# Attention and a feed-forward block on one core: three units of the first batch change their key layout, their loads and their order

## The chip, the cores and the metric

The kernel runs on one core of a Trainium2 chip. The metric is the device time of one execution in microseconds (us), lower is better. Beside the times there is a profile of one execution, taken by the hardware profiler. In it PE is TensorE's matmul stream and PEld its weight loads, DVE is VectorE, ACT is ScalarE, POOL is GpSimd and SP is SyncE. L190 is line 190 of the kernel before.

## The reference, cut to what matters

Eight sequences of 448 tokens go through attention with 12 heads of 64, and the result through two matrix products with a leaky ReLU between them. All inputs and the output are float32 (f32); the kernel computes in bfloat16 (bf16).

```python
scores = (q @ k.transpose(0, 1, 3, 2)) / sqrt(64)   # q, k, v: 8 x 12 x 448 x 64
attn   = exp(scores - max); attn = attn / (sum(attn) + 1e-9)
x      = (attn @ v).transpose(0, 2, 1, 3).reshape(3584, 768)
h      = x @ w_in                                   # w_in: 768 x 2048
out    = maximum(0.01 * h, h) @ w_out               # w_out: 2048 x 768
```

## The kernel before, in words

A unit is two heads of one sequence, so there are 48 units, six to a sequence (HP = 6). Units 0 to 5 are the first batch. A unit takes these steps.

- Load: q, k and v come from memory. `load_one` (L170) loads one tensor of one unit in f32 through SyncE's queue; `load_soft` (L153, its transfer on L163) loads one tensor of one or two units through GpSimd's queue and turns it into bf16 on the way. `load_w` (L211, L215) loads a slice of the weights, also through GpSimd's queue. Space for early loads comes from `rooms` (L134): slices of tiles that get their real contents only later (`w_in_mix`, `w_mix`, `o`, `deep_mix`, `c`).
- Cast: `cast` (L183) copies the raw tensor to the layout that the engines want: q and k to `qkb` (L190, for the new key layout L193 to L196), v to `v_old` (L198) or `v_sb` (L201 to L203). GpSimd does most casts. `qkb` has three places (unit number modulo 3).
- Turn: `transposes` (L294, matmuls against an identity on L301) brings q and k of a unit into `qkT`; VectorE copies the result out of PSUM (L305).
- Scores: `scores` (L311) multiplies keys by queries, one chunk of keys at a time; a chunk is one PSUM slot of three.
- Exponential: `expo` (L326, L331, L334, L336) runs on ScalarE, one instruction for a chunk.
- Weighted sum: `pv` (L366), through `pairs` (L355) or `weighted` (L340), multiplies the exponentials by v with a column of ones beside it; VectorE then takes the reciprocal of the sums (L374) and multiplies (L375). `x_transposes` (L379) puts the result into `xT` for the feed-forward part.

There are two key layouts. In the old one a unit's 448 keys are four chunks of 112, each with both heads: four exponentials of 112 partitions by 896 elements, 32 matmuls in the weighted sum. In the new one the first 384 keys are three chunks of 128 with both heads, and the last 64 keys of both heads share one chunk of 128 rows, so that its exponential has 448 elements and not 896; the weighted sum has 28 matmuls. Before the change units from HY = 18 on use the new layout and the first three sequences the old one.

The order of the first batch is written out by hand: `first(u)` (L863) for u from 0 to 5, with `supply(u)` (L851) as the list of casts and loads that GpSimd gets in that unit. Engines take their own instructions in order, so this list is GpSimd's order. After the first batch PE starts on the feed-forward part while later units' attention is placed in between: `part` (L416) and `head` (L783) multiply by `w_in` (L424), `mix_w_in` (L462, L473) makes sums of slices of `w_in` on VectorE, and a planner with a cost model (`place`, L1071) puts scores, turns (units 7 and 8 at first) and weighted sums between the products. The weights `w_in` come in three pieces of column blocks of 128: blocks 0 to 3, 4 to 9 and 10 to 15; below they are called piece one, two and three.

Of the kernel before, what the change touches and what calls it, by code (L numbers as in the profile page):

```python
# [16 lines left out]
def kernel(  # L17
# [9 lines left out]
    nc = tc.nc  # L27
# [100 lines left out]
    w_out_v = moe_w_out.rearrange("(ko ki) n -> ki ko n", ki=P)  # L128

    raw = {}  # L130

# [14 lines left out]
    def room(x, new):  # L146
# [4 lines left out]
        return rooms.pop(0)[:n].bitcast(F32).rearrange("p (h so d) -> p h so d", h=2, so=NSC)  # L151

    def load_soft(u, n, which):  # L153
        b, hp = divmod(u, HP)
        hs = slice(2 * hp, 2 * hp + 2 * n)
        for x in which:
            new = x > 0 and u >= HY
            t = room(x, new).rearrange("p h so d -> p (h so d)").bitcast(BF16)
            t = t.rearrange("p (u h so d) -> p u h so d", u=2, h=2, so=NSC)
            for p, so, keys in ((slice(0, D), NSC, slice(0, NSC * D)), (slice(D, P), KC, slice(NSC * D, S))) if new else (  # L160
                (slice(0, SC), NSC, slice(0, S)),
            ):
                nc.gpsimd.dma_start(  # L163
                    out=t[p, :n, :, :so].rearrange("p u h so d -> p (u h) (so d)"),
                    in_=(q, k, v)[x][b, hs, keys].rearrange("h (p so) d -> p h (so d)", so=so),
                )
            for i in range(n):
                raw.setdefault(u + i, {})[x] = t[:, i]

    def load_one(u, x, queue):  # L170
# [6 lines left out]
        raw.setdefault(u, {})[x] = t  # L177

    def load(u, parts=(0, 1, 2)):
        if u < NU and u % 2 == 0:  # L180
            load_soft(u, 2, parts)

    def cast(u, parts=(0, 1, 2), by=nc.gpsimd.tensor_copy):  # L183
        if u >= NU:
            return
        for x in parts:
            f = raw[u].pop(x)
            t = qkb[u % NB]
            if x < 2 and (x == 0 or u < HY):
                by(t[:SC, x].rearrange("p so h d -> p h so d"), f)  # L190
            elif x == 1:
# [4 lines left out]
                by(t[D:, 1, KC, 1], f[:D, 1, KC])  # L196
            elif u < HY:
                by(v_old[:, u % NV, :, :, :D], f)  # L198
            else:
                t = v_sb[u % NV]  # L200
                by(t[:, :2 * KC, :D].rearrange("p (h so) d -> p h so d", h=2), f[:, :, :KC])  # L201
# [9 lines left out]
    def load_w(n=1):  # L211
        for _ in range(n):
            if w_steps:
                o, i = w_steps.pop(0)
                nc.gpsimd.dma_start(out=o, in_=i)  # L215

    load_one(0, 1, nc.sync)
    load_one(0, 0, nc.sync)
# [47 lines left out]

    cast(0, (1,), both)
    cast(0, (0,), both)


# [23 lines left out]
    def transposes(u, bank=None):  # L294
        n = SC if u < HY else P
        t, flat = qkb[u % NB], qkT[u % NQ].rearrange("p i c s -> p (i c s)")[:, :2 * NSC * n]
# [14 lines left out]
    def scores(u, c):  # L311
        ps = next_slot()
        t = qkT[u % NQ]
        sc_t[u, c] = ps
        if u < HY:
            t = t.rearrange("p i c s -> p (i c s)")
# [9 lines left out]
    def expo(u, c):  # L326
        e, ps = e_sb[u % NE], sc_t.pop((u, c))
        n = SC if u < HY else P
        if c < KC:
            e = e[:n, :EM].rearrange("p (j c s) -> p j c s", j=2, c=KC)  # L330
            nc.scalar.activation(e[:, :, c, :], ps[:n, :, :S], AX.Exp, scale=scale)  # L331
        elif u < HY:
            e = e_old[u % NE][:n, :2 * S].rearrange("p (j s) -> p j s", j=2)
# [32 lines left out]
    def pv(u, j, bank=None):  # L366

        bank = next_bank() if bank is None else bank
        ps = bank[:, :NSC * (D + 1)].rearrange("p (q d) -> p q d", q=NSC)
        pairs(u, j, ps)  # L370
        if j == 0:
            x_t[u] = x_pool.tile([SC, NSC, 2, D], BF16, name="x")
        rec = r_pool.tile([SC, NSC, 1], F32, name="rec")
        nc.vector.reciprocal(rec, ps[:SC, :, D:])  # L374
        nc.vector.tensor_mul(  # L375
            x_t[u][:, :, j, :], ps[:SC, :, :D], rec.to_broadcast([SC, NSC, D])
        )

# [472 lines left out]
    def supply(u):  # L851

        for what, n, *parts in {0: [('load', 6, (0, 1)), ('qk', 3), ('v', 1), ('v', 2), ('load', 6, (2,))], 1: [('qk', 4), ('v', 3), ('load', 8, (0, 1))], 2: [('qk', 5), ('v', 4), ('w', 1)], 3: [('qk', 6), ('v', 5), ('w', 1)], 4: [('qk', 7), ('v', 6), ('load', 10, (0, 1)), ('load', 8, (2,))], 5: [('qk', 8), ('v', 7), ('load', 10, (2,)), ('load', 12)]}[u]:
            if what == "qk":
                cast(n, (0, 1))
            elif what == "v":
                cast(n, (2,))
# [5 lines left out]
    def first(u):  # L863
# [33 lines left out]


    transposes(0)
    cast(1, (0, 1), fast)  # L900
    for u in range(HP):
        first(u)
# [343 lines left out]
```

## Time and profile before

| what | value |
|---|---|
| median of 3 runs | 378.51 us (377.97, 378.51, 380.34) |
| the profiled execution, its time | 378.34 us |
| its span, first to last instruction | 376.6 us |
| TensorE clock granted | 0.999 |
| PE, ACT, DVE, POOL busy over the span | 98%, 69%, 68%, 51% |
| read from memory, written | 45.61 MB, 11.01 MB |

A busy share is an average over stages. The first 25 us (the first batch) and the time after it have different limits, so the stages are read apart. The profile says for each instruction what ended the idle time before it, with the sign "<-"; a second column of microseconds is the duration, and durations of pipelined instructions overlap, so that the distance from start to start is what a queue of them costs. A transfer issued by an engine shows there only as the time to issue it.

### The profile page before, as it was taken

How to read it: one execution, taken by the hardware profiler on the slowest of the kernel's cores; microseconds unless marked ns; L12 is line 12 of the kernel's file. 1: busy time of each engine (PE TensorE's matmuls, PEld its weight loads, DVE VectorE, ACT ScalarE, POOL GpSimd, SP SyncE). 2: the span in 40 equal slices, each digit the busy share in tenths (PEclk: the TensorE clock that was granted, in tenths of full speed). 3: DMA queues.
4: the chain of work that ended last, by engine and by line, in shares of the span. 5: the costliest groups of instructions: out<-in, count | busy, mean ns of one | idle time of the engine just before them, and what ended most of it. 6: DMA issues, size and time to landing. Idle time of an engine off the chain costs nothing.

```text
span 376.6 us, 10120 instructions
## 1 busy us (share of the span) xinstructions
PE 369.7 (98%) x4008; PEld 265.7 (71%) x4008; DVE 256.9 (68%) x558; ACT 259.6 (69%) x399; POOL 191.8 (51%) x376
## 2 busy tenths in 40 slices
PE   7999999999999999999999999999999999999996
PEld 3664658756698556996569966599665995679765
DVE  4765858778666867766676665775847775685763
ACT  5997885866768776758766587666787668636721
POOL 7985871986268989624588235792347020000000
PEclk9999999999999999999999999999999999999999
DMA  9999999999499885973869648798455740321123
GB/s 155 200 203 207 191 204 201 156 159 164 93 178 143 114 163 87 197 158 60 157 121 148 144 64 86 170 147 167 61 66 98 143 110 0 79 58 45 42 65 105
DMA packets 99600, 48.08 MB, mean 128 GB/s; under 512 B 64608, under 2 KB 96352, under 8 KB 99552
## 3 DMA queue, kind: packets, MB, share of 16 engines
q0 software_dynamic: 39600, 22.47, 44.6%
q1 hardware_dynamic: 59504, 24.50, 32.6%
q8 instruction: 31, 0.51, 0.6%
q10 hardware_dynamic: 448, 0.47, 0.4%
q14 instruction: 17, 0.14, 0.1%
HBM read 45.61 MB, written 11.01 MB: 150 GB/s over the span
## 4 chain that ended last, share of the span: by engine, by line
PE 94%; DMA 2%; DVE 1%; issue 1%; POOL 1%; ACT 1%; POOLq 0%; ACTq 0%; DVEq 0%
PE g L682 30%; PE g L548 14%; PE sc L548 14%; PE sc L322 7%; PE sc L350 6%; PE g L424 4%; PE sc L319 4%; PE sc L645 4%; PE sc L362 3%; PE g L817 2%; PE sc L343 2%; DMA w_in_mix<-in_v_dram 2%; PE g L362 1%; PE g L301 1%; PE sc L424 1%
## 5 line engine op out<-in xcount | busy, mean ns | idle before, releaser
L331 ACT ACTIVATE e<-sc 128x896 bf16<-128x896 f32 (+1 forms) x144 | 123.6, 923 | 30.7 <-PE sc L322 20.8
L682 PE MATMUL g<-w_out_sb,h 128*128 128x384 bf16 (+1 forms) x440 | 84.1, 325 | 0.0
L682 PEld LDWEIGHTS <-h 128*128 128x128 bf16 x592 | 54.4, 98 | 41.4 <-issue 11.2
L537 ACT ACTIVATE h<-c 128x512 bf16<-128x512 f32 (+1 forms) x72 | 43.1, 610 | 30.2 <-DVE c L563 12.4
L548 PEld LDWEIGHTS <-w_in_sb 128*128 128x128 bf16 x576 | 54.6, 98 | 5.7
L190 POOL COPY qkb<-fq 112x512 bf16<-112x512 bf16 x34 | 23.9, 703 | 41.6 <-DMA qkT<-qkb 32.5
L548 PEld LDWEIGHTS <-w_in_mix 128*128 128x128 bf16 x432 | 40.5, 98 | 3.7
L201 POOL COPY v<-fv 128x384 bf16<-128x384 bf16 x30 | 18.5, 617 | 43.1 <-PE sc L350 40.7
L687 DVE COPY o<-g 128x384 f32<-128x384 f32 x47 | 26.0, 553 | 13.7 <-PE g L682 13.5
L350 PE MATMUL sc<-v,e 128*128 128x65 bf16 x720 | 33.3, 193 | 0.0
L322 PE MATMUL sc<-qkT 64*128 64x448 bf16 (+1 forms) x210 | 32.8, 352 | 0.0
L350 PEld LDWEIGHTS <-e 128*128 128x128 bf16 x720 | 31.1, 98 | 1.3
L974 DVE RECIPROCAL rec<-sc 112x8 f32<-112x8 f32 x42 | 8.7, 207 | 33.6 <-PE sc L350 19.1
L975 DVE TENSOR_TENSOR x<-sc,rec 112x512 bf16<-112x512 f32 x42 | 29.0, 691 | 1.6 <-DVE rec L974 0.2
L548 PE MATMUL g<-xT,w_in_sb 128*128 128x256 bf16 (+1 forms) x216 | 28.5, 268 | 0.0
L548 PE MATMUL sc<-xT,w_in_sb 128*128 128x256 bf16 (+1 forms) x216 | 28.5, 268 | 0.0
L693 DVE TENSOR_TENSOR o<-o,g 128x384 f32<-128x384 f32 x39 | 21.4, 549 | 9.1 <-PE g L682 4.4
L343 PE MATMUL sc<-v,e 128*128 128x130 bf16 x120 | 26.5, 221 | 0.0
L649 DVE TENSOR_TENSOR o<-o,sc 128x192 f32<-128x192 f32 x39 | 13.7, 351 | 17.9 <-PE sc L645 17.9
L682 PE MATMUL g<-w_mix,h 128*128 128x384 bf16 x128 | 24.6, 326 | 0.2 <-DVE o L687 0.2
L163 POOL DMA_DIRECT2D fv<-in_v_dram x32 | 20.1, 641 | 7.7 <-DMA fq<-in_q_dram 3.1
L682 PE MATMUL g<-w_mix,hmix 128*128 128x384 bf16 x112 | 21.7, 326 | 0.0
(149 smaller groups left out, 744.1 us busy)
## 6 DMA issues: line engine op xcount, KB each, us to landing
fq<-in_q_dram POOLq DMA_DIRECT2D x17, 224.0 KB, 5.7
w_out_sb<-in_moe_w_out_dram POOLq DMA_DIRECT2D x4, 768.0 KB, 13.2
out_dram<-o SPq DMA_DIRECT2D x7, 336.0 KB, 3.4
w_in_sb<-in_moe_w_in_dram POOLq DMA_DIRECT2D x2, 1152.0 KB, 12.7
out_dram<-o SPq DMA_DIRECT2D x7, 288.0 KB, 3.4
fk<-in_k_dram POOLq DMA_DIRECT2D x15, 128.0 KB, 5.9
fv<-in_v_dram POOLq DMA_DIRECT2D x15, 128.0 KB, 4.8
out_dram<-o SPq DMA_DIRECT2D x7, 240.0 KB, 3.1
```

Source lines behind the costliest of these rows:

```text
L163: nc.gpsimd.dma_start(out=t[p, :n, :, :so].rearrange("p u h so d -> p (u h) (so d)"), in_=(q, k, v)[x][b, hs, keys].rearrange("h (p so) d ...
L190: by(t[:SC, x].rearrange("p so h d -> p h so d"), f)
L322: nc.tensor.matmul(ps[:, j, :S].rearrange("p (so s) -> p so s", so=NSC), t[p, 1, c], t[p, 0, :, :SC], start=True, stop=True,)
L331: nc.scalar.activation(e[:, :, c, :], ps[:n, :, :S], AX.Exp, scale=scale)
L343: nc.tensor.matmul(ps, e[:, EM + qc * SC:EM + qc * SC + P], vt[:, 2 * KC:].rearrange("p j d -> p (j d)"), start=True, stop=False, skip_gro ...
L350: nc.tensor.matmul(ps[:, j * (D + 1):(j + 1) * (D + 1)], e[:, at:at + P], vt[:, j * KC + c], start=False, stop=(c == KC - 1), skip_group_c ...
L537: nc.scalar.activation(hs[:, m:m + 2, cols], x.rearrange("p (m t) -> p m t", m=2), AX.Prelu, alpha=0.01)
L548: nc.tensor.matmul(ps[:, j * nh:(j + 1) * nh], w[:, kk, ts(j, P)], x[:, kk], start=(first and j == 0 and kk == 0), stop=(kk == KH - 1), sk ...
L682: nc.tensor.matmul(ps[:, cols], x[:, m], w[:, m], start=(first and m == 0), stop=(m == MH - 1), skip_group_check=True,)
L687: by(o[:, at], ps[:, :NW])
L693: nc.vector.tensor_add(o[:, at], o[:, at], ps[:, :NW])
L975: nc.vector.tensor_mul(x, ps[:, :, :, :D], rec.to_broadcast([SC, 2, 2 * NP, D]))
```

## The change: what it does

Units 3, 4 and 5 move to the new key layout (`old(u)` takes the place of `u < HY` in cast, turn, scores, exponential and weighted sum). Their k and v (k of units 3, 4, 5 and v of units 3, 4, 5) are no longer loaded by GpSimd in bf16; SyncE loads them in f32, in two transfers each, into six fixed places, three of which have first to be emptied of q and k of unit 0 and k of unit 1. GpSimd's opening loads shrink from nine tensors and piece one of `w_in` to six tensors; piece one has five column blocks and not four, and is issued in `supply(0)` behind the cast of unit 3's q and two loads. Units 1 to 5 turn the next unit's q and k ahead of the third and fourth scores and of the first weighted sum.

```diff
+    FIRST = 3
+    def old(u):
+        return u < FIRST or HP <= u < HY
...
+    split = ((slice(0, D), NSC, slice(0, NSC * D)), (slice(D, P), KC, slice(NSC * D, S)))
...
+    def load_into(u, x, t):
+        b, hp = divmod(u, HP)
+        for p, so, keys in split:
+            nc.sync.dma_start(
+                out=t[p, :, :so].rearrange("p h so d -> p h (so d)"),
+                in_=(q, k, v)[x][b, 2 * hp:2 * hp + 2, keys].rearrange("h (p so) d -> p h (so d)", so=so),
+            )
+        raw.setdefault(u, {})[x] = t
...
-    for lo, hi in ((0, 4), (4, 10), (10, MD)):
+    for lo, hi in ((0, 5), (5, 10), (10, MD)):
...
+    homes = [x.bitcast(F32).rearrange("p (h so d) -> p h so d", h=2, so=NSC) for x in rooms[:3] + rooms[9:12]]
+    del rooms[9:12]
     load_one(0, 1, nc.sync)
     load_one(0, 0, nc.sync)
     load_one(1, 1, nc.sync)
...
     load_soft(1, 1, (0,))
-    load_soft(2, 2, (0, 1))
+    load_soft(2, 2, (0,))
+    load_soft(2, 1, (1,))
     load_soft(0, 1, (2,))
     load_soft(1, 2, (2,))
-    load_soft(4, 2, (0, 1))
-    load_soft(3, 2, (2,))
-    load_soft(5, 1, (2,))
-    load_w(1)
+    load_soft(4, 2, (0,))
...
     cast(0, (1,), both)
     cast(0, (0,), both)
+    for u, x, y in ((3, 1, 0), (4, 1, 1), (5, 1, 3), (3, 2, 4), (4, 2, 5)):
+        load_into(u, x, homes[y])
...
-        pairs(u, j, ps)
...
+        if old(u):
+            pairs(u, j, ps)
+            x = x_t[u][:, :, j, :]
+        else:
+            n = 2 * (D + 1)
+            for y in range(NP):
+                weighted(u, j * NP + y, bank[:, y * n:(y + 1) * n])
+            x = x_t[u][:, j * NP:(j + 1) * NP].rearrange("p q j d -> p (q j) d")
...
-        ... {0: [('load', 6, (0, 1)), ('qk', 3), ('v', 1), ('v', 2), ('load', 6, (2,))],
-             1: [('qk', 4), ('v', 3), ('load', 8, (0, 1))], 2: [('qk', 5), ('v', 4), ('w', 1)],
-             3: [('qk', 6), ('v', 5), ('w', 1)], ...
+        ... {0: [('q', 3), ('load', 6, (0, 1)), ('w', 1), ('k', 3), ('v', 1), ('v', 2)],
+             1: [('qk', 4), ('load', 6, (2,)), ('v', 3)],
+             2: [('qk', 5), ('load', 8, (0, 1)), ('qk', 6), ('v', 4), ('w', 1)],
+             3: [('v', 5), ('w', 1)], ...
...
         if u >= 2:
             x_transposes(u - 2, next_bank())
-        if u == 1:
+        if u >= 1:
             transposes(u + 1)
-        if u >= 1:
-            pv(u - 1, 0)
         if u > 1:
             scores(u, 2)
             scores(u, 3)
-        if u != 1:
+        if u >= 1:
+            pv(u - 1, 0)
+        if u < 1:
             transposes(u + 1)
...
     transposes(0)
     cast(1, (0, 1), fast)
+    load_into(5, 2, homes[2])
     for u in range(HP):
         first(u)
```

More of the change, by code (lines that the diff above doesn't have):

```diff
@@ L157, in load_soft @@
             new = x > 0 and u >= HY
-            t = room(x, new).rearrange("p h so d -> p (h so d)").bitcast(BF16)
+            t = room(x, new)
+            t = t.rearrange("p h so d -> p (h so d)").bitcast(BF16)
             t = t.rearrange("p (u h so d) -> p u h so d", u=2, h=2, so=NSC)
-            for p, so, keys in ((slice(0, D), NSC, slice(0, NSC * D)), (slice(D, P), KC, slice(NSC * D, S))) if new else (
-                (slice(0, SC), NSC, slice(0, S)),
-            ):
+            for p, so, keys in split if new else ((slice(0, SC), NSC, slice(0, S)),):
                 nc.gpsimd.dma_start(
@@ L188, in cast @@
             t = qkb[u % NB]
-            if x < 2 and (x == 0 or u < HY):
+            if x < 2 and (x == 0 or old(u)):
                 by(t[:SC, x].rearrange("p so h d -> p h so d"), f)
@@ L314, in scores @@
         sc_t[u, c] = ps
-        if u < HY:
+        if old(u):
             t = t.rearrange("p i c s -> p (i c s)")
@@ L327, in expo @@
         e, ps = e_sb[u % NE], sc_t.pop((u, c))
-        n = SC if u < HY else P
+        n = SC if old(u) else P
         if c < KC:
```

15 lines of the change are left out of this document (8 added, 7 removed).

## The prediction

> **What bounds the kernel now.** I read the busy shares first, then busy time by stretches of 5 us, then the timelines of ACT, POOL and DVE over the first 40 us, the groups by form for prices, and last the DMA queues in short windows.
>
> ```profile
> PE 369.7 (98%) x4008; PEld 265.7 (71%) x4008; DVE 256.9 (68%) x558; ACT 259.6 (69%) x399; POOL 191.8 (51%) x376
> DMA  9999999999499885973869648798455740321123
> 10.00:15.00 5.00, 4.61 (x81) 3.07 (x79) 3.49 (x10) 5.00 (x8) 4.81 (x8) 1.00 1.42 197
> 15.00:20.00 5.00, 4.59 (x86) 3.11 (x84) 3.27 (x9) 5.00 (x7) 5.00 (x9) 1.00 1.32 203
> 20.00:25.00 5.00, 4.79 (x96) 3.49 (x93) 3.39 (x10) 5.00 (x7) 3.54 (x7) 1.00 1.40 200
> 25.00:30.00 5.00, 5.00 (x72) 3.01 (x70) 2.79 (x9) 3.77 (x5) 5.00 (x9) 1.00 1.16 211
> ```
>
> The first line is the whole span, the second the DMA engines in 40 slices of 9.4 us, the rest are stretches (busy us of PE, PEld, DVE, ACT, POOL; clock; DMA share; GB/s). ACT is busy 5.00 of 5 us from 10 to 25 us; after that PE is, and stays so to the end. POOL is full from 15 to 20 us, and the DMA engines never rest in the first 100 us. So the first batch ends when ACT has done its exponentials, and all time after it is PE's, unless something is late.
>
> ```profile
> 9.93 2.55 ACT L331 ACTIVATE e<-sc 112x896 bf16<-112x896 f32 x3
> ...
> 25.20 1.01 ACT L334 ACTIVATE c<-sc 112x896 bf16<-112x896 f32 x1
> 26.38 1.72 ACT L331 ACTIVATE e<-sc 112x896 bf16<-112x896 f32 x2 [0.16 <-PE sc L319]
> L331 ACT ACTIVATE e<-sc 128x896 bf16<-128x896 f32 x90 | 76.1, 918 | 20.8 <-PE sc L322 20.8
> L336 ACT ACTIVATE e<-sc 128x448 bf16<-128x448 f32 x30 | 16.5, 552 | 1.6
> ```
>
> ACT's timeline and two groups. From 9.93 to 25.20 us are 19 exponentials, 0.804 us from start to start, without a gap over 0.13. A chunk of 896 elements is 918 ns, one of 448 is 552.
>
> ```profile
> 9.06 0.85 POOL L215 DMA_DIRECT2D w_in_sb<-in_moe_w_in_dram  x1 [0.41 <-DMA w_in_mix<-in_q_dram]
> 11.59 1.17 POOL L190 COPY qkb<-w_in_mix 112x512 bf16<-112x512 bf16 x2
> 27.83 1.17 POOL L190 COPY qkb<-w_mix 112x512 bf16<-112x512 bf16 x2
> 38.04 0.96 POOL L190 COPY qkb<-w_mix 112x512 bf16<-112x512 bf16 x1 [4.23 <-DMA w_mix<-in_q_dram]
> L194 POOL COPY qkb<-fk 128x384 bf16<-128x384 bf16 x30 | 16.9, 565 | 1.5 <-DMA fk<-in_k_dram 1.5
> L195 POOL COPY qkb<-fk 64x64 bf16<-64x64 bf16 x30 | 8.9, 296 | 0.0
> L201 POOL COPY v<-fv 128x384 bf16<-128x384 bf16 x30 | 18.5, 617 | 43.1 <-PE sc L350 40.7 <-DMA fv<-in_v_dram 1.2
> ```
>
> POOL's timeline: the issue of piece one at 9.06, the first casts, the casts of unit 8's q and k (27.83 to 28.94), and the first long wait, 4.23 us for a load, at 38. Two casts in 1.11 us (11.59 to 12.70) are 0.555 us each. The groups are the new layout's copies.
>
> ```profile
> 36.78 0.56 DVE L473 TENSOR_TENSOR w_in_mix<-w_in_sb 128x768 bf16<-128x768 bf16 x1 [2.56 <-DMA w_in_sb<-in_moe_w_in_dram]
> 38.92 0.21 DVE L974 RECIPROCAL rec<-sc 112x8 f32<-112x8 f32 x1 [0.39 <-ACT e L331]
> ```
>
> ```profile
> 30.52 0.40 PE g L301 x8
> ```
>
> DVE's timeline: it waits 2.56 us for piece three of `w_in` and soon after takes a weighted sum out of PSUM. The last line, from the chain of waits, is PE's turn of unit 8.
>
> **Part by part.** *ACT.* Three exponentials of 896 become 448: 3 x (918 - 552) = 1.10 us off the stage that ACT bounds. This is the gain.
>
> *PE.* A chunk with 64 keys of both heads is one matmul and not two, a weighted sum 28 and not 32, turns are 128 wide and not 112. PE has 0.2 to 0.4 us to spare in each 5 us of the batch (rows above); behind it only unit 5's weighted sum is shorter, by at most 4 of 32 matmuls that take 1.03 us together, 0.13. Nothing taken. The turn moved forward (0.51 to 0.57 us for 8 matmuls) holds back scores 3 and 4: in unit 2 they would start at 14.3 and not 14.19, while ACT needs them at 14.70. Cost 0; if ACT's lead were gone, up to 0.5 a unit. It removes three waits of PE for DVE's copy (0.8 us together), of which ACT saw one gap of 0.13. DVE's copy grows from 0.62 to 0.62 x 1024 / 896 = 0.71, hidden in DVE's 1.5 idle us of 5.
>
> *SP.* Twelve more issues of about 0.45 us (rows of SP's three loads) from 4.1 us on. The transposes behind them start only at 39.88, so the queue costs nothing; what they do to the DMA engines is next.
>
> *DMA.* The same bytes are read. Six tensors of 0.229 MB are now written in f32, in 1536 packets for 1344. GpSimd's queue alone moves 1578 packets in 4 us (10 to 14 us), 394 a us, so 3.4 us of engine time goes. SyncE's queue alone moved 174 in the half us from 3.0, 348 a us, and 250 a us over 2 to 4: 4.4 to 6.1 us come. Were reads the limit (394 packets of 1 KB a us for GpSimd), it would be 3.4 again. So 0 to 2.7 us more work for the DMA engines; I take 1.0, by SyncE's own best row.
>
> ```profile
> q0 software_dynamic: 681, 0.34, 88.6%
> q1 hardware_dynamic: 178, 0.17, 23.5%
> q0 software_dynamic: 1578, 0.78, 144.8%
> ```
>
> The first two lines are 4 to 7 us, where both queues had work, the third 10 to 14 us. The new loads start at about 5 us, beside q and k of unit 2 and v of unit 0, which lands at 10.54 and is on the early chain. Ahead of it lie 1120 packets of GpSimd's queue for 1344 (k of unit 3 has left), of which 235 were moved by 5.5 us. If the queues take equal turns for the other 885, as many new packets come between: 2005 for 1344, 661 / 394 = 1.7 us later. At the 4 to 1 of those rows it is 1341, no delay. PE has about 0.25 us of lead there (scores at 12.57 to 12.85, exponential at 13.11), so ACT loses 0 to 1.45 us. I take 0.4, nearer the row.
>
> *POOL.* Each of units 3, 4, 5 needs a memset (198 ns) and three copies for k, 198 + 501 + 230 + 232 = 1.16 us for 0.555, and three for v, 506 + 230 + 234 = 0.97 for 0.555: 3.07 us more by the medians, 4.63 by the means, which hold the time lost beside DVE. The f32 source has no POOL row; the nearest are DVE's casts (420 ns for f32, 290 for bf16 at 512 elements) and POOL's own equal rate an element; I take equal. The three issues saved (0.7 each) lie ahead of 8.7 us. What counts is the queue from piece one to unit 8's cast: 28.94 - 9.06 = 19.88 us, 1.74 of it idle, so 18.14 of work, which becomes 21.2 to 22.8. It now starts with the cast of unit 3's q, as its load lands: 9.0 us if the new loads cost it nothing (the issue at 9.06 waited for it), 437 / 394 = 1.1 later with equal turns. So unit 8's cast ends between 30.2 and 32.9; I take 9.5 + 21.8 = 31.3, nearer the medians. PE turns unit 8 at 30.52 now, and with ACT's 1.10 less 0.4 would come at 29.8. PE waits there: **0.8 us later than before**, between 0.3 earlier and 2.4 later. This holds no wait of POOL's own for a load or for PE.
>
> *Piece three.* POOL issues piece two behind the same longer queue, at about 23 to 26 us and not 19.23. It lands at 31.0 now; less 1.5 us from last byte to landing (v of unit 0 shows that) and 1.18 MB at 205 GB/s, 5.75 us, its bytes start at 23.8. With a longer piece one ahead (0.197 MB, 1.0 us) they could start at 24.8, and with 1.4 us from issue to first bytes they are there at 24.4 to 27.4. So piece three lands 0 to 2.7 us after its 36.75, by the DMA work or by the late issue, whichever is longer; I take 1.0. DVE's sum waits for it; the take-out of PSUM has 0.39 us to spare (38.53 to 38.92) and PE's next scores another 0.3. So PE is 0.7 early to 2.0 late there, with 1.0 it is 0.3 late. It comes after the turn of unit 8 and is less, so it adds nothing.
>
> Sum: ACT's chain reaches the end of the batch 0.7 us early, POOL's queue gives it back and 0.8 more: 378.34 + 0.8 = 379.1 us for the profiled execution, which is 0.17 under the median of the three runs, and I leave the forecast at **379.1**.
>
> The three issues that POOL is spared stand at nothing in this sum, because POOL's timeline shows it idle just there, 0.78 us before 7.98 and 0.41 before 9.06. The Trainium skill (DMA: Bandwidth & Descriptors, Rules for kernel authors) says that spreading transfers over the issuing engines does not help bandwidth, as all use the same 16 engines, and saves issue time alone. By that rule POOL would gain 3 x 0.70 = 2.1 us, unit 8's cast would end at 29.2 and the sum would be the first rival's 377.7. The trace speaks against it here: the time saved falls into a wait.
>
> **The rivals.** *Faster.* POOL keeps up: q of unit 3 lands by 9, the copies run at their medians or faster, and unit 8's cast ends before PE comes. For it: 21.2 us of work from 9.0 is 30.2. Then ACT's 1.10 stands until piece three, whose 0.69 us of slack caps it: 378.34 - 0.69 = 377.7. It decides at 30.5 us, the end of unit 8's cast; against it is POOL's 5.00 of 5 already.
>
> *The new loads are late.* At the slowest shares (178 packets in 3 us, or 281 in the 3 us from 41, beside GpSimd's queue), k of 3, 4, 5 and v of 3 are 1024 packets and need 11 to 17 us from 5.2 on, with 1.5 to land up to 24. POOL comes to v of unit 3 at 16.5 to 18 and stands there, with k of unit 5 behind it; PE then turns unit 5 some 3 us late and ACT starves. Price 2.5 to 5 us: about 382. Against it: the 178 may be a queue that drained, as k of unit 1 had no more; with equal turns v of unit 3 is there by 14. The Trainium skill (same page, Queues, rings and completion order) says that an engine goes round its queues packet by packet and that a packet holds several descriptors. By that rule GpSimd's joined rows get the larger share and the time would be this rival's 382; the 4 to 1 row bears it out only if that queue had not drained.
>
> *The change does not do what it says.* V of unit 0 lands 1.35 us late, ACT's 1.10 is gone at once, and POOL is just in time for PE at its old place: 378.3.
>
> **How the numbers follow.** POOL's queue 0.45, faster 0.27, late loads 0.15, nothing 0.13. The time is that of the first. Its own range is 378.3 to 380.5. The range for 8 in 10 leaves out a third of the faster case and half of the late one: 377.4 to 381.8. About 1% (3.8 us) is what a measurement of this kernel can tell from no change. Only the late loads reach 382.3, at half their chance, 0.07; within 1% 0.91; faster 0.02, for a mechanism that I have missed, since ACT's gain is capped at 1.1.
>
> **What would show it.** ACT has 21 exponentials of 896 and 3 of 448 for the batch, still 0.80 apart, if its chain holds. PE's wait at the turn of unit 8, for POOL, is the forecast; none there and 377.7 the first rival. POOL waiting for a load by SyncE is the second. A DVE wait for `w_in` longer than 2.56 us shows piece three late. I am wrong if POOL's f32 copies differ much from the bf16 ones, or the DMA shares do.

## The result, and the profile after

The changed kernel took 380.24 us (median of 22 runs, 378.97 to 383.68), the kernel before in the same sessions 378.06 us (22 runs, 377.74 to 380.34). The ratio is 1.006, 95% interval 1.0044 to 1.0076: **0.6% slower**, within the 1% that the prediction called "same" and inside its range, but 1.1 us above its 379.1. The profiled execution of the changed kernel took 380.10 us with a span of 378.3 us, 1.7 us longer than the one of before. Below, L206, L210 to L212 and L217 to L219 are the casts of the changed kernel, L231 is `load_w`, L319 the turn, L349, L352 and L354 the exponentials, L496 the sums of `w_in`, L1000 and L1001 the take-out of a weighted sum, L447 the product with `w_in`.

First the busy shares and the stretches of 5 us (columns as before: stretch, busy us of PE, PEld, DVE, ACT, POOL, clock, DMA share, GB/s).

```profile
PE 369.6 (98%) x3993; PEld 265.7 (70%) x3993; DVE 258.2 (68%) x558; ACT 259.2 (69%) x399; POOL 191.3 (51%) x388
...
10.00:15.00 5.00, 4.75 (x93) 3.65 (x92) 3.01 (x9) 5.00 (x7) 3.69 (x8) 1.00 1.28 245
15.00:20.00 5.00, 4.43 (x75) 3.03 (x71) 3.35 (x10) 4.97 (x8) 4.66 (x14) 1.00 1.23 232
20.00:25.00 5.00, 4.87 (x83) 3.39 (x81) 3.39 (x10) 4.68 (x7) 4.85 (x11) 1.00 1.31 202
25.00:30.00 5.00, 5.00 (x64) 2.90 (x60) 2.67 (x10) 3.03 (x4) 4.90 (x10) 1.00 1.18 178
30.00:35.00 5.00, 4.48 (x31) 2.02 (x30) 3.44 (x5) 3.35 (x6) 5.00 (x10) 1.00 1.17 210
```

ACT is no longer full from 20 us on. PE is as busy as before up to 30 us, but from 30 to 35 us it is busy for 4.48 us, where it was full (the last row; the same stretch of the kernel before stands below). The DMA engines write more bytes than before from 10 to 20 us (245 and 232 GB/s for 197 and 203; SyncE's loads arrive in f32, with twice the bytes a number) and less from 25 to 30 us (178 for 211).

```profile
30.00:35.00 5.00, 5.00 (x37) 2.40 (x34) 3.76 (x5) 4.01 (x8) 3.81 (x6) 1.00 1.16 212
```

ACT's timeline (start, duration, line, count, and in brackets the idle time ahead of it with what ended it):

```profile
15.95 2.60 ACT L349 ACTIVATE e<-sc 128x896 bf16<-128x896 f32 x3
18.34 0.65 ACT L354 ACTIVATE e<-sc 128x448 bf16<-128x448 f32 x1
19.02 2.72 ACT L349 ACTIVATE e<-sc 128x896 bf16<-128x896 f32 x3
21.63 0.54 ACT L354 ACTIVATE e<-sc 128x448 bf16<-128x448 f32 x1
22.41 2.54 ACT L349 ACTIVATE e<-sc 128x896 bf16<-128x896 f32 x3 [0.24 <-PE sc L340]
24.82 0.56 ACT L354 ACTIVATE e<-sc 128x448 bf16<-128x448 f32 x1
26.21 1.72 ACT L349 ACTIVATE e<-sc 112x896 bf16<-112x896 f32 x2 [0.82 <-PE sc L337]
```

The three short exponentials are there. But units 3 and 4 take 3.07 and 3.39 us from start to start (it was 3.20 and 3.19), and after the batch ACT waits 0.82 us for PE's next scores, where it waited 0.16 before.

POOL's timeline, with the waits and the steps that the prediction dated:

```profile
8.61 0.61 POOL L206 COPY qkb<-w_in_mix 112x512 bf16<-112x512 bf16 x1 [2.87 <-DMA w_in_mix<-in_q_dram]
...
11.70 0.50 POOL L210 CAST qkb<-w_in_mix 128x384 bf16<-128x384 f32 x1
12.15 0.23 POOL L211 CAST qkb<-w_in_mix 64x64 bf16<-64x64 f32 x1
...
15.05 0.61 POOL L206 COPY qkb<-w_in_mix 112x512 bf16<-112x512 bf16 x1 [1.16 <-DVE rec L399]
...
23.55 0.84 POOL L231 DMA_DIRECT2D w_in_sb<-in_moe_w_in_dram  x1
...
25.35 0.83 POOL L231 DMA_DIRECT2D w_in_sb<-in_moe_w_in_dram  x1
...
30.00 1.17 POOL L206 COPY qkb<-w_mix 112x512 bf16<-112x512 bf16 x2
```

Unit 8's cast ends at 31.17 (29.00 before). The f32 copies take what the bf16 ones take (0.50 and 0.23 us). POOL waits 2.87 us for q of unit 3 and 1.16 us ahead of q of unit 4. The row puts the 1.16 us down to DVE, but the load of q of units 4 and 5, by GpSimd's own queue, was issued at 5.00 and landed at 14.90, 0.15 us before that cast starts; in the kernel before it was issued at 5.07 and landed at 12.89. In this execution POOL does not wait for a load by SyncE. Pieces two and three are issued at 23.55 and 25.35 (19.23 and 23.25 before). The load of q of units 4 and 5, with the us from issue to landing, in the changed kernel and then in the kernel before:

```profile
w_in_mix<-in_q_dram POOLq DMA_DIRECT2D x1, 224.0 KB, 9.9
```

```profile
w_in_mix<-in_q_dram POOLq DMA_DIRECT2D x1, 224.0 KB, 7.8
```

PE's timeline at three places, and DVE's at the second of them:

```profile
30.68 0.37 PE L319 MATMUL g<-ident,qkb 112*128 112x112 bf16 x4 [0.34 <-POOL qkb L206]
31.22 0.37 PE L319 MATMUL g<-ident,qkb 112*128 112x112 bf16 x4 [0.18 <-POOL qkb L206]
...
41.36 0.37 PE L337 MATMUL sc<-qkT 64*128 64x448 bf16 x2 [0.52 <-DVE x L1001]
...
78.27 0.81 PE L705 MATMUL g<-w_mix,h 128*128 128x384 bf16 x4 [0.46 <-DVE o L710]
```

```profile
38.65 0.56 DVE L496 TENSOR_TENSOR w_in_mix<-w_in_sb 128x768 bf16<-128x768 bf16 x1 [3.17 <-DMA w_in_sb<-in_moe_w_in_dram]
39.31 1.15 DVE L496 TENSOR_TENSOR w_in_mix<-w_in_sb,w_in_mix 128x768 bf16<-128x768 bf16 x2
40.38 0.20 DVE L1000 RECIPROCAL rec<-sc 112x8 f32<-112x8 f32 x1
40.61 0.69 DVE L1001 TENSOR_TENSOR x<-sc,rec 112x512 bf16<-112x512 f32 x1
```

Unit 8's turn waits for POOL, as forecast. Then piece three lands at 38.65 and not 36.75, and DVE stands in front of its sum. The take-out of the weighted sum stands behind that sum in DVE's queue, and PE's scores need the PSUM slot that it empties.

How late the changed kernel is, followed through the span by ACT's leaky ReLUs, which are the same in both kernels (start after less start before): +0.57 us at 39 us, +1.28 from 46 to 72 us, +2.06 at 122 us, and 1.68 near the end. PE's own events give the steps: part(0,0) starts at 24.90 (25.06 before, 0.16 early), the turn of unit 7 at 29.39 (29.59), the product behind unit 8's turn at 31.43 (30.86, 0.57 late), the weighted sum behind piece three at 42.80 (41.53, 1.27 late). So in this execution POOL cost 0.77, piece three another 0.70, and 0.8 came near 78 us, where nothing was forecast.

### The profile page after: what moved, and what is told of

Same layout as the page of the kernel before. It is cut to its first block, busy times and chain, and to the rows that moved or that the text cites. A ratio compares the mean times of both kernels' runs of the same rounds, so it can differ in the third digit from the quotient of the medians.

```text
span 378.3 us, 10123 instructions
## 1 busy us (share of the span) xinstructions
PE 369.6 (98%) x3993; PEld 265.7 (70%) x3993; DVE 258.2 (68%) x558; ACT 259.2 (69%) x399; POOL 191.3 (51%) x388
## 4 chain that ended last, share of the span: by engine, by line
PE 93%; DVE 2%; DMA 2%; POOL 1%; issue 1%; ACT 0%; POOLq 0%; ACTq 0%
PE g L705 30%; PE sc L571 14%; PE g L571 14%; PE sc L340 7%; PE sc L368 6%; PE g L447 4%; PE sc L668 4%; PE sc L337 3%; PE sc L380 3%; PE g L840 2%; PE sc L361 2%; DMA w_in_mix<-in_q_dram 2%; PE g L319 1%; DVE x L400 1%; PE g L380 1%
## 5 line engine op out<-in xcount | busy, mean ns | idle before, releaser
L349 ACT ACTIVATE e<-sc 128x896 bf16<-128x896 f32 (+1 forms) x144 | 123.7, 922 | 32.1 <-PE sc L340 20.9
L206 POOL COPY qkb<-fq 112x512 bf16<-112x512 bf16 x34 | 22.3, 657 | 44.2 <-DMA qkT<-qkb 35.0
L217 POOL COPY v<-fv 128x384 bf16<-128x384 bf16 x30 | 17.7, 591 | 41.6 <-PE sc L368 39.2
L340 PE MATMUL sc<-qkT 64*128 64x448 bf16 (+1 forms) x231 | 36.4, 353 | 0.0
L368 PEld LDWEIGHTS <-e 128*128 128x128 bf16 x792 | 34.3, 98 | 1.4
L1000 DVE RECIPROCAL rec<-sc 112x8 f32<-112x8 f32 x42 | 8.7, 206 | 34.0 <-PE sc L368 21.4
L1001 DVE TENSOR_TENSOR x<-sc,rec 112x512 bf16<-112x512 f32 x42 | 29.0, 691 | 1.4
L716 DVE TENSOR_TENSOR o<-o,g 128x384 f32<-128x384 f32 x39 | 21.4, 549 | 9.6 <-PE g L705 4.6
```

The source lines that it names most:

```text
L340: nc.tensor.matmul(ps[:, j, :S].rearrange("p (so s) -> p so s", so=NSC), t[p, 1, c], t[p, 0, :, :SC], start=True, stop=True,)
L368: nc.tensor.matmul(ps[:, j * (D + 1):(j + 1) * (D + 1)], e[:, at:at + P], vt[:, j * KC + c], start=False, stop=(c == KC - 1), skip_group_c ...
L716: nc.vector.tensor_add(o[:, at], o[:, at], ps[:, :NW])
L1001: nc.vector.tensor_mul(x, ps[:, :, :, :D], rec.to_broadcast([SC, 2, 2 * NP, D]))
```

## The experiments

Three theories were to be told apart. T1: POOL's longer queue. T2: the DMA engines, which write six tensors in f32 and so bring piece three late. T3: the new order of PE's work in the batch. All ratios are against the kernel before, measured beside it, with 95% intervals; its median lay between 377.91 and 377.99.

The profiled executions begin at slightly different times, since the first loads do not land alike (the first exponential starts at 6.72 us in the profile of before, at 5.99 to 6.64 in the others). This table therefore gives, for one profiled execution each, the start of ACT's leaky ReLUs less that in the profile of before, less the same difference of the first exponential: how much a kernel has lost since then.

| kernel | at 39 us | at 47 us | at 67 us | at 122 us | ratio |
|---|---|---|---|---|---|
| changed | 0.99 | 1.70 | 1.70 | 2.48 | 1.0060 |
| old order | 2.21 | 2.97 | 2.97 | 3.76 | 1.0058 |
| before, new order alone | 0.10 | 0.10 | 0.11 | 0.08 | 1.0001 |
| loads alone | 0.23 | 0.51 | 0.51 | 1.47 | 1.0035 |
| no small copies | -0.08 | 1.33 | 1.33 | 1.66 | 1.0038 |
| k first | -0.14 | 1.13 | 1.14 | 1.46 | 1.0048 |
| no loads of unit 5 | -0.01 | 0.95 | 0.96 | 1.28 | 1.0043 |
| sums later | 0.15 | 0.16 | 0.81 | 0.79 | 1.0036 |
| sums later, k first | 0.26 | 0.26 | 0.90 | 2.08 | 1.0034 |
| before, sums later | 0.00 | 0.00 | 0.60 | 0.58 | 1.0024 |

The column at 39 us holds POOL's part, the step to 47 us piece three's, the step to 67 us (it lies between 47 and 50) is told with the sums, and the step to 122 us lies at 78. Single executions scatter, however: up to 38 us the kernel "sums later" does what the changed kernel does, and it has lost 0.15 us at 39 us, not 0.99; the kernel of experiment 8, also the same up to there, has lost 0.70. A difference of less than 0.8 us between two rows shows nothing by itself.

### 1. The old order in the changed kernel

```diff
-        if u >= 1:
+        if u == 1:
             transposes(u + 1)
+        if u >= 1:
+            pv(u - 1, 0)
         if u > 1:
             scores(u, 2)
             scores(u, 3)
-        if u >= 1:
-            pv(u - 1, 0)
-        if u < 1:
+        if u != 1:
             transposes(u + 1)
```

> The changed kernel with the old order of the first batch: the next unit is turned behind scores 3 and 4 and the first weighted sum, everything else as changed. Theories: T1, VectorE is not the cause, POOL's longer queue is (it makes PE's turn of unit 8 late and issues pieces two and three of w_in late); T2, the f32 writes make the DMA engines late with piece three; T3, the new order makes PE wait (for DVE's product, 0.8 us in three units) and so wastes the 0.8 us of the 1.10 that ACT was spared. T1 and T2: 380.1 us within 0.3, ratio to the kernel before 1.005 or more, as unit 8's cast and piece three come no earlier. T3: part(0,0) of PE starts 0.4 to 0.8 us earlier than its 24.90, 379.3 to 379.7, if what is behind it can follow. Slower than 380.4 would say that the new order is needed with the smaller units.

Measured: 379.87 us (378.96 to 382.40, 8 runs), ratio 1.0058 (1.0034 to 1.0082), as with the new order. Its profiled execution, 1.4 us above its median, loses more in the batch (PE waits 1.15 us for v of unit 3 by POOL at 24.8 us; POOL had waited 1.12 us for SyncE's load of it, which landed at 18.40). T3 falls from this side: taking the new order away does not bring the time back.

### 2. The new order alone

The same edit the other way round, in the kernel before.

> The kernel before, with nothing changed but the order of the first batch (next unit turned ahead of scores 3 and 4 and of the first weighted sum). T1 and T2: no difference, 378.3 within 0.3, ratio 0.999 to 1.001, since neither POOL nor the DMA engines get more work. T3: PE's cycle in the batch stretches from 3.13 us a unit towards 3.4, ACT gets gaps, 378.8 to 379.2.

Measured: 378.08 us (377.61 to 378.64, 11 runs), ratio 1.0001 (0.9992 to 1.0010). T3 falls from this side too, and the prediction's price of 0 for the order stands.

### 3. The small copies on VectorE

```diff
-                by(t[:D, 1, KC, 0], f[:D, 0, KC])
-                by(t[D:, 1, KC, 1], f[:D, 1, KC])
+                few = nc.vector.tensor_copy if u < HP else by
+                few(t[:D, 1, KC, 0], f[:D, 0, KC])
+                few(t[D:, 1, KC, 1], f[:D, 1, KC])
...
-                by(t[:D, 2 * KC, :D], f[:D, 0, KC])
-                by(t[D:, 2 * KC + 1, :D], f[:D, 1, KC])
+                few = nc.vector.tensor_copy if u < HP else by
+                few(t[:D, 2 * KC, :D], f[:D, 0, KC])
+                few(t[D:, 2 * KC + 1, :D], f[:D, 1, KC])
```

> The changed kernel, with the four small copies (64 x 64) that each of units 3 to 5 needs moved from GpSimd to VectorE: twelve copies of 0.23 us, 2.8 us less in POOL's queue, 12 copies of about 0.1 to 0.15 us more for DVE. T1: unit 8's cast ends near 28.5 and not 31.17, PE's turn of unit 8 has no wait for POOL, pieces two and three are issued 2 us earlier and piece three lands near 36.8: 378.0 to 378.9, ratio 0.999 to 1.002. T2: piece three still lands at 38.65, 379.7 to 380.1. T3: no gain, and DVE's busier queue makes it 380.1 to 380.6.

Measured: 387.23 us (386.63 to 388.18, 4 runs), ratio 1.0244 (1.0228 to 1.0260). None of the theories expected that, because the edit does something else. In DVE's timeline of this kernel the moved copies stand behind POOL's memset of the same rows, and everything of DVE stands behind them:

```profile
11.57 0.46 DVE L212 CAST qkb<-w_in_mix 64x64 bf16<-64x64 f32 x1 [1.62 <-POOL qkb L209]
...
15.94 0.54 DVE L212 CAST qkb<-w_in_mix 64x64 bf16<-64x64 f32 x1 [2.48 <-POOL qkb L209]
```

PE's waits over the first 60 us (in all, times, longest) show who paid:

```profile
PE g L414 <- DVE x L402: 6.7, 3, 5.0
```

Twelve copies of 0.2 us were moved to an engine with 1.5 idle us of 5, and cost 9 us: an in-order queue took over the other engine's lateness. As a test of T1 it says nothing.

### 4. The loads alone

```diff
-    FIRST = 3
+    FIRST = 6
...
-        for p, so, keys in split:
+        t = t[:SC]
+        for p, so, keys in ((slice(0, SC), NSC, slice(0, S)),):
             nc.sync.dma_start(
```

> The changed kernel with units 3 to 5 in the old layout (112 keys a chunk): their k and v are still loaded in f32 by SyncE, but cast in one copy each, with the old exponentials. POOL has the work of before, ACT does not gain its 1.10 us, the DMA engines have all the new work. T1: 378.1 to 378.6, ratio within 0.001 of 1. T2: piece three lands at 38 or later and the time is 379.3 to 379.9. T3: 378.8 to 379.2, as this has the new order too.

Measured: 379.17 us (378.40 to 380.58, 9 runs), ratio 1.0035 (1.0021 to 1.0049). More than half of the loss is there without the new layout and without a longer copy on POOL; T1 alone would have had 1.000. But this kernel keeps the new lists of casts and loads and the larger piece one too, and no run takes these back, so the loss is not shown to be that of the f32 writes alone. By the table its profile loses 0.28 us to piece three, which lands 31.23 us after the first exponential (30.61 in the kernel with the new order alone, a difference within the scatter told below), and 0.96 at 78 us.

### 5. Without the small copies

The four copies of the last 64 keys are skipped for units 3 to 5.

```diff
-                by(t[:D, 1, KC, 0], f[:D, 0, KC])
-                by(t[D:, 1, KC, 1], f[:D, 1, KC])
+                if u >= HP:
+                    by(t[:D, 1, KC, 0], f[:D, 0, KC])
+                    by(t[D:, 1, KC, 1], f[:D, 1, KC])
...
-                by(t[:D, 2 * KC, :D], f[:D, 0, KC])
-                by(t[D:, 2 * KC + 1, :D], f[:D, 1, KC])
+                if u >= HP:
+                    by(t[:D, 2 * KC, :D], f[:D, 0, KC])
+                    by(t[D:, 2 * KC + 1, :D], f[:D, 1, KC])
```

> The changed kernel without the twelve small copies (64 x 64) of units 3 to 5 on POOL: the last 64 keys of each head in these units are left at zero, so part of the computation is left out. Nothing takes the copies' place on another engine. POOL has 12 x 0.23 = 2.8 us less between unit 3's q and unit 8's cast. T1 (POOL's length): unit 8's cast ends near 28.5, PE's turn of unit 8 has no wait, pieces two and three are issued 1.4 to 2.5 us earlier: 378.0 to 378.8, ratio at most 1.002. T2 (the DMA engines' f32 writes): piece three still lands near 38.6 and the time is 379.2 or more, ratio 1.003 or more, as with the loads alone.

Measured: 379.28 us (378.49 to 379.62, 5 runs), ratio 1.0038 (1.0026 to 1.0050), T2's number. Unit 8's turn has no wait, and the table shows nothing lost at 39 us. But pieces two and three, issued at 21.16 and 22.44 and so 2.4 and 2.9 us earlier, do not land earlier. POOL still waits 1.14 us for the load of q of unit 4, and 0.53 us for SyncE's load of k of unit 3. PE's and DVE's timelines of this kernel:

```profile
41.12 0.37 PE L339 MATMUL sc<-qkT 64*128 64x448 bf16 x2 [1.23 <-DVE x L1003]
```

```profile
38.48 0.56 DVE L498 TENSOR_TENSOR w_in_mix<-w_in_sb 128x768 bf16<-128x768 bf16 x1 [3.18 <-DMA w_in_sb<-in_moe_w_in_dram]
```

PE, early now, waits 1.23 us where it waited 0.52. What POOL gives back, piece three takes: two limits in a row, of which the later one decides.

### 6. k of unit 4 ahead of its q

```diff
-1: [('qk', 4), ('load', 6, (2,)), ('v', 3)]
+1: [('k', 4), ('q', 4), ('load', 6, (2,)), ('v', 3)]
```

> The changed kernel with k of unit 4 cast ahead of its q on POOL. POOL stands idle for 1.16 us at 15.05 ahead of q of unit 4, while k of unit 4, by SyncE, needs 1.16 us of copies. If k is there by then, POOL's queue behind it is about 1.1 us shorter: T1 expects unit 8's cast to end near 30.1 and the time at 379.2 to 379.6; T2 expects no change, 380.1 within 0.3. If k of unit 4 has not landed by 15, the wait only changes its name and the time stays.

Measured: 379.75 us (378.71 to 380.42, 6 runs), ratio 1.0048 (1.0034 to 1.0062). The means go T1's way, but the interval overlaps that of the changed kernel. The trace is clear about POOL. It goes from v of unit 2 straight to k of unit 4 and its 1.16 us of idling are gone; unit 8's cast starts at 28.51 and PE's turn has no wait. Then the same place takes it back:

```profile
29.63 0.56 PE L319 MATMUL g<-ident,qkb 112*128 112x112 bf16 x8
...
40.62 0.36 PE L337 MATMUL sc<-qkT 64*128 64x448 bf16 x2 [1.09 <-DVE x L1001]
```

Piece three lands at 37.91, issued at 23.85: 31.78 us after the first exponential, 0.57 less than in the changed kernel. That is no more than single executions scatter: with POOL's list unchanged it is 31.7 and 31.6 us in the profiles of experiments 8 and 9, and with k first once more it is 32.5 in that of experiment 11. So this run does not show that a part of piece three's lateness is POOL's. What it does show is that PE's wait at unit 8's turn goes away when POOL's wait for q of unit 4 does.

### 7. Pieces two and three early

```diff
-2: [('qk', 5), ('load', 8, (0, 1)), ('qk', 6), ('v', 4), ('w', 1)], 3: [('v', 5), ('w', 1)]
+2: [('w', 1), ('qk', 5), ('load', 8, (0, 1)), ('w', 1), ('qk', 6), ('v', 4)], 3: [('v', 5)]
```

> The changed kernel with POOL's issues of pieces two and three of w_in moved ahead, to the start of the third unit's work and behind the next load there: some 4 us earlier, at the price of later issues of nothing else. If piece three is late because POOL issues it late, it lands at 36.9 or earlier and the time falls to 379.2 to 379.5, with PE's wait for unit 8 left in. If the DMA engines are what makes it late (T2), it lands near 38.6 all the same, no change: 380.1 within 0.3; the next units' loads, now behind the pieces in the queue, could make it 380.4.

Measured: 381.86 us (379.95 to 383.33, 6 runs), ratio 1.0103 (1.0079 to 1.0127). Its profiled execution is the slowest of the six. With the pieces issued at 18.03 and 21.94, piece three was still waited for until 39.07. What had stood ahead of the pieces now stood behind them, q and k of unit 8, for which POOL and then PE waited. POOL's timeline, then PE's:

```profile
32.25 0.62 POOL L206 COPY qkb<-w_mix 112x512 bf16<-112x512 bf16 x1 [2.44 <-DMA w_mix<-in_q_dram]
33.43 0.62 POOL L206 COPY qkb<-w_mix 112x512 bf16<-112x512 bf16 x1 [0.56 <-DMA w_mix<-in_k_dram]
```

```profile
32.92 0.37 PE L319 MATMUL g<-ident,qkb 112*128 112x112 bf16 x4 [1.51 <-POOL qkb L206]
34.10 0.37 PE L319 MATMUL g<-ident,qkb 112*128 112x112 bf16 x4 [0.81 <-POOL qkb L206]
```

This fits a shared limit in the DMA engines up to 39 us, where an order only chooses who is late; the run does not prove it. T2 expected no change to 380.4, and was too kind.

### 8. The take-out ahead of the difference

```diff
-            nc.vector.tensor_sub(h[:, lo, one], h[:, lo, two], h[:, lo, one])
             short = cuts[i + 1] - cuts[i] < 4 * P
             keep(o1, left, b, idle if c == 0 and short else calm)
+            nc.vector.tensor_sub(h[:, lo, one], h[:, lo, two], h[:, lo, one])
```

> The changed kernel with one pair of VectorE's instructions exchanged in the output stage: the first product is taken out of PSUM ahead of the difference of h, not behind it. In the trace this difference took 2.24 us at 75.5 (0.69 us elsewhere), from the start to the end of a run of POOL's copies, and PE waited 0.46 us at 78.3 for the take-out behind it; in the kernel before it began later in that run, took 1.45 us, and PE did not wait. If that is a cost of its own, 379.6 to 379.8; if PE's lead absorbs it, no change, 380.1 within 0.2.

Measured: 379.92 us (379.34 to 380.84, 5 runs), ratio 1.0065 (1.0052 to 1.0078): no gain. PE's wait for the take-out is gone, and 0.7 us later PE waits 0.41 us for another product of DVE, which now stands behind the same long difference (1.77 us). Its profile still loses 0.81 us there. The exchange only moves the wait.

### 9. The sums of piece three later

VectorE's sums are handed out by a table: block number of `w_in`, sums behind it.

```diff
-{5: 3, 6: 3, 7: 2, 8: 1, 9: 2, 10: 1}
+{5: 3, 7: 3, 8: 2, 9: 2, 10: 2}
```

> The changed kernel with VectorE's three sums that read piece three of w_in put behind the next weighted sum's reciprocal and product (and the later sums one group up), nothing else. Piece three itself lands as late as in the changed kernel, near 38.6, but PE's scores no longer stand behind it by way of VectorE's queue. If piece three costs time through that queue, PE's wait for VectorE's x at 41.36 (0.52 us) is gone, part of PE's later start too: 379.2 to 379.7. What is left is POOL's part. If the time stays at 380.1 within 0.3, piece three's lateness is a sign and not the cause.

Measured: 379.36 us (378.22 to 380.72, 12 runs), ratio 1.0036 (1.0023 to 1.0050), 0.9 us better than the changed kernel's 380.24 in another session. In the table the step from 39 to 47 us is gone (0.15 to 0.16, where the changed kernel has 0.99 to 1.70). So piece three cost time by way of DVE's queue, not by its lateness alone: in experiment 6 it lands as late after the first exponential (31.8 us, here 31.6), and there 1.27 us are lost. That little is lost at 39 us already is not the edit's doing; in this execution PE waited for POOL only 0.18 us at unit 8's turn. Then 0.65 us are lost again between 47 and 50 us, which the next run explains.

### 10. The same in the kernel before

> The kernel before with the same three sums of VectorE put behind the next reciprocal and product: the control. There piece three landed at 36.75 and VectorE had 0.39 us to spare behind it, so no gain is expected: 378.0 within 0.2, ratio 0.9995 to 1.0005. A gain of 0.3 us or more would say that the kernel before lost time there as well.

Measured: 378.54 us (377.73 to 383.53, 12 runs), ratio 1.0024 (1.0003 to 1.0044, without the longest run), 0.6 us worse and not within 0.2. Eight runs lie between 377.73 and 378.83 and four at 380.39 or more, so the price is uncertain. Its profile loses 0.60 us in the same place as experiment 9. PE's timeline of this control:

```profile
47.87 0.37 PE L319 MATMUL sc<-qkT 64*128 64x448 bf16 x2 [0.42 <-DVE x L975]
```

The later sums crowd the next take-out but one. So experiment 9 carries about 0.6 us of its own, and the two ratios with the sums later, 1.0036 and 1.0024, leave about 0.5 us for all else in the change; their intervals overlap.

### 11. Sums later and k first

> The last kernel together with k of unit 4 cast ahead of its q, which took PE's wait for POOL at unit 8's turn away and left one wait of 1.1 us for VectorE's x behind piece three. With both gone nothing is late in the first 45 us, and ACT's shorter exponentials should show: 377.4 to 378.4, ratio 0.997 to 1.002. If the time stays above 379.2, the loss is in neither place.

Measured: 379.33 us (378.29 to 380.35, 12 runs), ratio 1.0034 (1.0022 to 1.0045), nothing better than experiment 9. The expectation of 377.4 to 378.4 was wrong: of the 1.4 us left, 0.6 is the sums' own price, and the profiled execution loses 1.18 us at 78 us (PE waits 0.9 us for the take-out there). Nor was all of the early loss gone: PE still waits 0.18 us for POOL at unit 8's turn, POOL 0.68 us for SyncE's load of k of unit 3. Above all, no gain of ACT's appears at 39 us.

### 12. Without the loads of unit 5

```diff
-    for u, x, y in ((3, 1, 0), (4, 1, 1), (5, 1, 3), (3, 2, 4), (4, 2, 5)):
+    for u, x, y in ((3, 1, 0), (4, 1, 1), (3, 2, 4), (4, 2, 5)):
         load_into(u, x, homes[y])
+    raw[5][1] = homes[1]
...
-    load_into(5, 2, homes[2])
+    raw[5][2] = homes[5]
```

> The changed kernel without SyncE's four loads of k and v of unit 5, whose casts read unit 4's tensors, so that part of the computation is left out: 512 packets and 0.46 MB of writes less for the DMA engines, with POOL's queue and all else unchanged. T2 (the DMA engines make piece three late): it lands 1 us or more earlier, near 37.5, no wait of PE behind it, and the time is 379.2 to 379.7 (POOL's wait at unit 8 is left). If piece three is late because POOL issues it late (25.35), it lands near 38.6 all the same: 380.1 within 0.3.

Measured: 379.68 us (379.08 to 380.46, 6 runs), ratio 1.0043 (1.0028 to 1.0059), the upper end of T2's band. Piece three lands at 38.20, 31.67 us after the first exponential for 32.35: 0.7 us earlier, less than the 1 us expected, and no earlier than in experiment 9, which has all the loads (31.6). PE still waits 0.78 us behind it. PE's wait for POOL at unit 8 went too (q of unit 3 came sooner and POOL ran 0.5 us ahead), which was not meant, so the run does not separate T2.

No version beat the kernel before. Not tried: a sum table that clears both take-outs, and one or two units in the new layout instead of three.

## Why the prediction was right, and where it was not

The time fell into the range, and the verdict "within 1%" held, but the term that gave the number was right partly by luck, two others were wrong, and one loss nobody had listed.

- **POOL's queue: the forecast held, its make-up partly by luck.** Forecast: unit 8's cast ends at 31.3 and PE's turn is 0.8 us late. Measured: 31.17, and PE 0.57 us late behind it after being 0.20 early ahead of it, 0.77 in all. But the forecast was a start at 9.5 and 21.8 us of work, and "holds no wait of POOL's own for a load". Measured are a start at 8.61, 21.4 us of work and the wait of 1.16 us for q of unit 4. Without that wait the cast would have ended at 30.0, before PE came to the turn at 30.34, and PE would not have waited: the first rival's condition. The wait comes with the new loads. The load of q of units 4 and 5, which GpSimd's queue makes in all kernels, lands at 12.1 to 12.9 in the three profiles without SyncE's f32 loads and at 14.1 to 15.1 in the eleven with them. Experiment 6 gives POOL work for that time, and PE's wait at the turn is gone. So the longer queue alone does not make PE late; the queue and the late load together do.
- **ACT's gain: mis-sized, and it hardly reached PE.** "3 x (918 - 552) = 1.10 us" takes durations, which overlap. From start to start a chunk of 896 costs 0.80 us (the prediction's own number) and one of 448 costs 0.54 where nothing holds the next (18.62 to 19.16 in experiment 9), so the term is 3 x 0.26 = 0.8. And with it ACT no longer sets the pace. PE was credited with 0.2 to 0.4 idle us in each 5 as spare room, "nothing taken"; in the changed kernel PE's waits from 15 us to its first product with `w_in`, part(0,0), are 0.28 and 0.29 us for DVE's x and none for ACT, while ACT waits 0.82 us for PE at 26 us. From the first exponential to part(0,0) it is 18.34 us before, 18.44 and 18.33 in experiments 2 and 10 (old layout too), 18.60 in the changed kernel, and 18.18 to 18.31 in experiments 5, 6, 9, 11 and 12. So 0.02 to 0.26 us of the 1.10 reach PE. A further limit lay close behind, which the prediction did not date: piece one, which part(0,0) needs, landed at 19.63 before, but at 24.24 in the changed kernel, 0.66 us ahead of part(0,0), and 0.04 us ahead of it in experiment 5.
- **v of unit 0: did not occur.** Taken at 0.4 us. VectorE casts it at 9.63 in the changed kernel and at 10.57 before: it came earlier.
- **Piece three: the step that failed.** "With 1.0 it is 0.3 late. It comes after the turn of unit 8 and is less, so it adds nothing." It landed 1.9 us late (within the 0 to 2.7 given) and so added 0.70 us behind unit 8's turn. Experiments 5 and 6 show that the two stand in a row: with POOL's part gone, piece three alone makes PE lose 1.3 to 1.4 us. Experiment 9 shows that the loss goes through DVE's queue. What makes piece three late stays open. By the landings it comes 30.0, 30.6 and 31.3 us after the first exponential in the three profiles without the new loads (before, experiments 2 and 10), 31.2 with SyncE's loads alone, and 31.6 to 32.5 in the changed kernel and experiments 5, 6, 8, 9, 11 and 12. So it comes later in the changed kernel and its variants, but with the loads alone no later than in the control of experiment 10. The first three differ by 1.3 us among themselves, and the changed kernel from experiments 8 and 9, whose loads and lists for POOL are the same, by 0.6 and 0.7; that is too much to split the 1.9 us between the f32 writes, the new lists and the later issue.
- **A loss at 78 us: not forecast.** 0.8 us in the changed kernel's profile; told below.
- **The rivals.** "Faster" needed unit 8's cast before 30.5; experiments 5, 6 and 12 met that condition and were still slower, since piece three's 0.69 us of slack was gone. "Late loads" was wrong in its price: POOL waits for SyncE not at all in the changed kernel's profile, 0.2 to 0.7 us for k of unit 3 in those of experiments 1, 5, 8, 11 and 12, and 1.12 us for v of unit 3 in that of experiment 1, not the 2.5 to 5 us of that rival. "Does not do what it says" named a late v of unit 0, which did not come. Of the Trainium skill's two rules weighed there, the one on spreading (DMA: Bandwidth & Descriptors, Rules for kernel authors) agrees with the trace: from 10 to 14 us the two queues together brought 0.68 MB in f32 and 0.32 MB in bf16, 0.33 million numbers, where before GpSimd's queue alone brought 0.78 MB in bf16, 0.39 million. The issue time saved fell into POOL's wait of 2.87 us.

The forecast of 379.1 for the profiled execution stands against 380.10. The difference, 1.0 us, is about piece three's 0.70 and the 0.8 at 78 us, less what other places gave back (the lag falls from 2.06 to 1.68 us between 122 us and the end).

## What to carry to other kernels

Where durations overlap, cost a chunk by the distance of starts, and ask which engine, and which load, ends the stage once the first limit is gone. Limits that follow one another on the same path do not add: remove the first and read how much the second takes back before calling it a gain. Before a small operation is moved to an idle engine, ask what it waits for: in an in-order queue everything behind it inherits that wait. Before a difference between two profiled executions is read as an effect, look how far two executions of the same code lie apart; here it was up to 0.8 us at 39 us.

## What the runs showed of the hardware

**A DVE subtraction stretched by POOL's copies.** The same subtraction (128x1024 bf16) takes 0.69 us when POOL is quiet. At 75 us in the changed kernel it begins just after POOL's run of copies does; DVE's timeline, then POOL's:

```profile
75.52 2.24 DVE L720 TENSOR_TENSOR h<-h 128x1024 bf16<-128x1024 bf16 x1 [1.60 <-PE g L705]
77.68 0.54 DVE L710 COPY o<-g 128x384 f32<-128x384 f32 x1
...
79.91 0.69 DVE L728 TENSOR_TENSOR h<-h 128x1024 bf16<-128x1024 bf16 x1
```

```profile
75.44 0.67 POOL L206 COPY qkb<-fq 112x512 bf16<-112x512 bf16 x1
75.99 0.66 POOL L206 COPY qkb<-fk 112x512 bf16<-112x512 bf16 x1
76.55 0.66 POOL L214 COPY x_mix<-fv 112x512 bf16<-112x512 bf16 x1
77.10 1.12 POOL L206 COPY qkb<-fq 112x512 bf16<-112x512 bf16 x1
```

It ends at 77.76, during the fourth copy, which itself takes 1.12 us for 0.66. How long depends on where in the run it starts: 1.22 us with the new order alone and 1.45 before (no loss at 78 us, or a wait under 0.2), 1.78 without the small copies (0.33 lost), 2.24 here and 2.42 with the loads alone (0.8 and 0.96 lost). So a shift of less than a microsecond between two engines decides over 0 to 1 us at a place that the change does not touch. The Trainium skill (SBUF — State Buffer, Who interferes with whom) says that DVE and GpSimd share ports under an exclusive lock. The trace fits that: the subtraction's last 0.69 us begin at 77.07, as the third copy gives way to the fourth, and the fourth is longer by 0.46. But DVE here seems to wait over three copies in a row, 1.55 us, and not one of 0.66.

**How SyncE's and GpSimd's queues share the DMA engines.** Packets, MB and share, first for 5 to 8 us, then for 10 to 14 us of the changed kernel:

```profile
q0 software_dynamic: 917, 0.45, 117.7%
q1 hardware_dynamic: 69, 0.06, 9.0%
```

```profile
q1 hardware_dynamic: 860, 0.68, 67.2%
q0 software_dynamic: 647, 0.32, 58.6%
```

SyncE issued its twelve loads from 4.13 to 13.95 us, 0.6 us or more apart (the prediction took 0.45). In the first stretch, with the first five of them issued and none landed, its queue gets 1 packet in 14; from 10 to 14 us, with GpSimd's queue thinner, more than half. So a low share of SyncE's queue, as in the profile of before, need not mean a drained queue, as the prediction had held possible. The loads still were in time for POOL in this execution; that the share rose as GpSimd's queue ran thin fits this, but no run tests it.

**Spread.** Single runs of the kernels with SyncE's f32 loads lie 1.1 to 4.7 us apart, those of the kernel before 1.2 to 2.6 in the four sessions; one profiled execution of the former can lie 1.5 us off its median. But the control of experiment 10, without these loads, spreads over 5.8 us, so the loads are not shown to be the cause.
